# A spectral mixer with a gated token MLP on one core: the order and width of the channel transforms that interrupt the second matrix product

## The chip, the cores and the metric

The kernel runs on one core of one Trainium2 chip. The metric is the device time of one execution in microseconds, as the median of several. The profile is of one execution, taken by the hardware profiler; its times count from the first instruction. TensorE (PE, with its weight loads as PEld), VectorE (DVE), ScalarE (ACT) and GpSimd (POOL) are the engines that compute; SyncE (SP) and POOL issue most of the DMAs.

## What is computed

The input x has 2048 tokens of 512 channels, all in fp32. It is normalized per token, and two branches start from the result.

```python
xn = _layernorm(x, axis=-1)
# branch A: a filter in the 2D spectrum
X = jnp.fft.rfft2(xn, axes=(-2, -1)) * (w_r + 1j * w_i)
s = jnp.fft.irfft2(X, s=(S, D), axes=(-2, -1))
# branch B: an MLP over the tokens
h = _layernorm(xn, axis=-1)
u = gelu(jnp.einsum("bsd,sf->bdf", h, w1) + b1)          # F = 1792
y = jnp.einsum("bdf,fs->bds", u, w2) + b2
g = silu(y.transpose(0, 2, 1))
return x + s * g
```

Here `S` is 2048, `D` is 512, and the two weights of the MLP are 2048x1792 and 1792x2048.

## The kernel before

The Fourier transforms are matrix products with small constant matrices. The kernel has three stages on TensorE, which follow each other without a pause:

- up to about 84 us the first part of the first MLP product, with the forward token transform between its matmuls;
- up to about 204 us the rest of that product, with the channel transform, the filter and the first step of the way back, eight steps of `filter_pair`; what is left of the spectral branch then stands in the tile `ey`;
- from 204.47 us the second MLP product, with the last two transforms of the spectral branch.

The change is in the third stage. Tokens are worked off in eight pairs p of 128-token blocks, `j0 = p` and `j1 = p + 8` (loop `for p in range(NP)` near the end). Each pair is computed with Strassen's scheme in seven products, in the order `ORDER = (1, 2, 5, 6, 3, 7, 4)` (line 802). `products(p, n)` (line 906) issues 21 matmuls of 128x128 weights and 256 columns: three for each of seven slices of the hidden dimension, because each fp32 operand is split into a high and a low part. The weights are the tiles `w2f`, which ACT (high part) and DVE (low part) make in `w2_forms`, two or so products ahead; the moving tiles `fa`, `fb`, `fc`, `fd` are combinations of the hidden layer, made earlier. Three PSUM banks take the results (`banks`, line 903): `bx` for products 1, 6, 7 and 4, which accumulate there one after the other, `by` and `bz` for the rest. Between them the bank is read: `c22`, for instance, is the sum of `bx` after product 7 and of an earlier copy `p5`; product 4 then goes on accumulating in `bx`. DVE makes such sums (`summed`, tile `c`), and ACT makes the gates from them (`gate`, tile `g`).

Behind one product of each pair (`k == slot`; k = 5, that is product 7, in pairs 0 to 6, and k = 3, product 6, in the last) the products are interrupted by transforms of the spectral branch. A string of letters in `PARTS` says which, and in what order:

- `E`, `even_channels` (line 966): the even channel frequencies as 32 matmuls of 64x64 (weights `yt`, moving `ci`, which the profile calls `cd`);
- `O`, `odd_channels` (line 977): the odd ones as 8 matmuls of 128x128;
- `F`, `channels` (line 984): even and odd ones as 16 matmuls of 128x128, even ones then at full width also;
- `S`, `spectral` (line 1019): the last token transform, of the pair before, as 8 matmuls of 64x512 (weights `y`, moving `cft`).

`E`, `O` and `F` write banks 6 and 7, `S` writes banks 0 and 1. Their weights `yt` are gathered from `ey` by ACT and DVE (`gathered`) in steps named "g" in the plan `SLOTS`. After the interruption `unfolded(p)` (line 991) makes `y` from banks 6 and 7 in three steps: the first right behind it, the others at the places marked "s" in the plan. If the letters of the pair hold an "E", its first step is one copy of 257 columns on ACT, three short DVE operations and two long ones; otherwise it is one copy of 512 columns on ACT and two long DVE operations. From the second pair on, `finish` (line 1035) multiplies the result of `S` with the gates on DVE, and POOL adds the rows to `out` with accumulating DMAs; `sums_of_blocks` then forms the next weight blocks on DVE.

Nearly all instructions stand in program order on each engine, which the class `Kept` sees to (line 140 in the profile is its helper, so most rows of this stage carry L140). The letters are read here:

```python
                if k == slot:
                    for part in PARTS[p]:
                        {"S": spectral, "E": even_channels, "O": odd_channels, "F": channels}[part](p - (part == "S"))
                    yts.pop(p)
                    pieces = unfolded(p)
                    if p:
                        for g, j in zip(gates.pop(p - 1), (j0 - 1, j1 - 1)):
                            finish(g, j, whole)
```

Of the kernel before, what the change touches and what calls it, by code (L numbers as in the profile page):

```python
# [17 lines left out]
S, D, F = 2048, 512, 1792  # L18
# [22 lines left out]

PARTS = ("EO", "OES", *["ESO"] * 5, "SF")

KD = np.concatenate([np.arange(0, 256, 4), np.arange(2, 256, 4), np.arange(1, 256, 2)])

# [95 lines left out]
def spectral_mixer_kernel(tc, x, w1, b1, w2, b2, wk, we, wx, c_f, c_ft, c_d, c_i, c_g, c_h, c_t, out):  # L143
# [19 lines left out]
    with tc.tile_pool(name="ps", bufs=1, space=PSUM) as psp, ExitStack() as left, ExitStack() as right:  # L163
# [827 lines left out]
        def unfolded(p):  # L991

            es, y = new_sums(p) if p else first_sums
            e0, e1 = (es[:, :, k].rearrange("p i b c -> p i (b c)") for k in range(2))
            if "E" in PARTS[p]:
                first, odd = ps[:, 6, :256].rearrange("p (i s c) -> p i s c", s=2, c=64), ps[:, 6:8, 256:]
# [53 lines left out]
        for p in range(NP):  # L1050
# [8 lines left out]
            for k, n in enumerate(ORDER):  # L1059
# [23 lines left out]
# [3 lines that stand above are left out]
# [57 lines left out]
```

## Time and profile before

| | |
|---|---|
| median of 3 runs | 366.80 us (366.69 to 366.90) |
| the profiled execution's own time | 367.48 us |
| its span, first to last instruction | 365.70 us |
| granted TensorE clock | 1.00 |
| TensorE busy | 359.3 us, 98% of the span |
| VectorE busy | 304.8 us, 83% |
| ScalarE busy | 210.1 us, 57% |
| first product of the third stage | starts at 204.47 us |
| interruption of the first pair | starts at 219.40 us |
| interruption of the second pair | starts at 238.51 us |

A row of the order of time reads: start, length, engine, line, operation, output tile <- input tiles, shape, count. A row merges neighbours of one group, so its length runs from the start of the first to the modelled end of the last; matmuls are pipelined, and a matmul's own duration is longer than the distance to the next one. That is why the text works with differences of starts. Where a row merges two shapes, it shows the first.

### The profile page before, as it was taken

Reading aid. Unit: us, or ns where it says so; the run is one execution under the profiler, and the core shown is the slowest. Engines: PE = TensorE matmul, PEld = TensorE weight load, DVE = VectorE, ACT = ScalarE, POOL = GpSimd, SP = SyncE. Lnnn points to the kernel's source line nnn. Section 1 sums busy time; section 2 is a strip of 40 time slices with the busy share of each in tenths; the row PEclk is TensorE's granted clock in tenths of the full one; section 3 lists DMA queues with packets and bytes.
Section 4 is the critical chain, followed back from the end, with each engine's and each line's share of the span. In section 5 each row is a group of like instructions: output and inputs, shape, how many; then the busy total and the mean of one; then the engine's idle time right before and its main releaser. Section 6 shows DMA issues by size and latency. Waiting matters only on the chain.

```text
span 365.7 us, 8778 instructions
## 1 busy us (share of the span) xinstructions
PE 359.3 (98%) x3442; PEld 309.5 (85%) x3442; DVE 304.8 (83%) x586; ACT 210.1 (57%) x383; POOL 87.1 (24%) x134
## 2 busy tenths in 40 slices
PE   8999999999999999999999999999999999999994
PEld 5788888888777787777888999989898989898983
DVE  5899999947689997999995978787787969696983
ACT  4877677768634425765426875646464545565541
POOL 4233333323221022220111001050403122140330
PEclk9999999999999999999999999999999999999999
DMA  6988899305694676986568278698898989898623
GB/s 203 243 199 203 206 266 343 140 2 135 148 293 183 208 217 181 266 240 208 169 210 194 100 196 204 163 190 207 187 186 215 177 222 159 233 159 232 106 33 83
DMA packets 33449, 68.66 MB, mean 188 GB/s; under 512 B 4768, under 2 KB 19536, under 8 KB 33280
## 3 DMA queue, kind: packets, MB, share of 16 engines
q1 hardware_dynamic: 24432, 42.44, 41.3%
q0 software_dynamic: 8496, 25.01, 31.9%
q10 hardware_dynamic: 480, 0.66, 0.6%
q8 instruction: 27, 0.44, 0.5%
q14 instruction: 14, 0.11, 0.1%
HBM read 59.70 MB, written 8.13 MB: 185 GB/s over the span
## 4 chain that ended last, share of the span: by engine, by line
PE 97%; DVE 1%; DMA 1%; ACT 0%; issue 0%
PE ps L140 97%; DMA x<-in_x_dram 1%; DVE rows L140 0%; DVE stm L245 0%; ACT g L140 0%; DVE h L273 0%; DVE tm L230 0%; ACT sdm L224 0%; DVE mvm L221 0%; DVE nbm L238 0%; DVE rsm L231 0%; DVE r0m L229 0%; DVE v2m L222 0%; DVE v2m L223 0%
## 5 line engine op out<-in xcount | busy, mean ns | idle before, releaser
L140 PE MATMUL ps<-h,w1h 128*128 128x512 f32 x400 | 117.5, 401 | 0.3 <-DVE nbm L238 0.3
L140 PEld LDWEIGHTS ps<-h,w1h 128*128 128x128 f32 x400 | 73.7, 190 | 20.1 <-issue 4.9
L140 PE MATMUL ps<-h,w1l 128*128 128x512 f32 x200 | 68.0, 392 | 0.0
L140 DVE TENSOR_TENSOR w2f<-a,w2f 128x896 fp32r<-128x896 f32 x36 | 39.2, 1089 | 22.0 <-ACT w2f L140 22.0
L140 PEld LDWEIGHTS ps<-h,w1l 128*128 128x128 f32 x200 | 38.0, 190 | 8.3
L140 ACT ACTIVATE w2f<-a 128x896 fp32r<-128x896 f32 x36 | 36.8, 1022 | 12.5 <-PE ps L140 7.9
L140 PE MATMUL ps<-fb,w2f 128*128 128x256 f32 x336 | 41.7, 279 | 0.0
L140 POOL DMA_DIRECT2D s<-in_w_dram x14 | 18.3, 1310 | 96.9 <-DMA s<-in_w_dram 49.0
L140 PE MATMUL ps<-fa,w2f 128*128 128x256 f32 x336 | 41.1, 277 | 0.0
L140 PEld LDWEIGHTS ps<-fb,w2f 128*128 128x128 f32 x336 | 39.6, 188 | 1.7 <-ACT g L140 0.8
L140 PE MATMUL ps<-fc,w2f 128*128 128x256 f32 x336 | 39.8, 277 | 0.0
L140 PEld LDWEIGHTS ps<-fa,w2f 128*128 128x128 f32 x336 | 39.6, 188 | 0.0
L140 PEld LDWEIGHTS ps<-fc,w2f 128*128 128x128 f32 x336 | 39.0, 188 | 0.0
L140 POOL DMA_DIRECT2D out_dram<-r x28 | 23.6, 1278 | 27.6 <-DVE r L140 27.6
L156 ACT ACTIVATE w1h<-w1s 128x512 fp32r<-128x512 f32 x26 | 16.1, 631 | 23.6 <-PE ps L140 10.0
L309 POOL TENSOR_TENSOR ey<-t 128x256 f32<-128x256 f32 x16 | 15.7, 980 | 45.4 <-DVE t L307 45.4
L669 POOL DMA_DIRECT2D xc<-xc x16 | 9.8, 619 | 68.5 <-ACT xc L667 44.8
L140 ACT ACTIVATE w2f<-s 128x896 fp32r<-128x896 f32 x15 | 15.3, 1022 | 13.5 <-PE ps L140 12.5
L471 DVE TENSOR_TENSOR w1l<-w1r,w1h 128x384 fp32r<-128x384 f32 x32 | 20.7, 652 | 0.8 <-ACT w1h L468 0.8
L140 PE MATMUL ps<-fd,w2f 128*128 128x256 f32 x168 | 20.5, 277 | 0.0
L140 ACT ACTIVATE g<-c,b2t 128x256 f32<-128x256 f32 x24 | 12.1, 504 | 14.6 <-DVE c L140 14.6
L269 ACT ACTIVATE h<-x,nbm,rsm 128x256 f32<-128x256 f32 (+1 forms) x34 | 18.3, 591 | 3.5 <-DVE nbm L264 2.5
(132 smaller groups left out, 603.0 us busy)
## 6 DMA issues: line engine op xcount, KB each, us to landing
a<-in_w_dram SPq DMA_DIRECT2D x22, 448.0 KB, 4.1
wt<-in_wk_dram POOLq DMA_DIRECT2D x16, 512.0 KB, 5.6
s<-in_w_dram SPq DMA_DIRECT2D x16, 448.0 KB, 4.3
s<-in_w_dram POOLq DMA_DIRECT2D x16, 448.0 KB, 6.3
w1s<-in_w_dram SPq DMA_DIRECT2D x52, 128.0 KB, 4.1
w1r<-in_w_dram SPq DMA_DIRECT2D x28, 192.0 KB, 5.3
xc<-xc POOLq DMA_DIRECT2D x16, 256.0 KB, 3.0
out_dram<-in_x_dram SPq DMA_DIRECT2D x4, 960.0 KB, 6.9
```

Source lines behind the costliest of these rows:

```text
L140: return lambda *args, **kw: self.keep(operation(*args, **kw))
L156: return A.activation(hi, src, AF.Copy), V.tensor_sub(lo, src, hi.bitcast(F32))
L269: keep(A.activation(to, v, AF.Identity, bias=m["nb"][:, i], scale=m["rs"][:, i, 1:2]))
L309: G.tensor_add(ey[:, 0::3, :, j], a, b)
L471: keep(V.tensor_sub(dst, src, hi.bitcast(F32)))
L669: keep(G.dma_start(*(v.rearrange("p s t c -> p s (t c)") for v in (there[c::2], here[1 - c::2, ::-1]))))
```

## The change

One line. The first pair gets full-width channel transforms (`F`) in place of even, then odd ones (`EO`); the second pair gets even, spectral, odd (`ESO`), as the third to seventh pairs have, in place of odd, even, spectral (`OES`).

```diff
-PARTS = ("EO", "OES", *["ESO"] * 5, "SF")
+PARTS = ("F", *["ESO"] * 6, "SF")
```

With "F" the first pair has no "E" among its letters, so its `unfolded` takes the other branch:

```python
            if "E" in PARTS[p]:
                ...
            else:
                pe = ps[:, 6:8].rearrange("p i (h k) -> p i h k", h=2)
                A.activation(e1, pe[:, :, 1], AF.Copy)
                V.tensor_add(e0, pe[:, :, 0], e1)
                V.tensor_sub(e1, pe[:, :, 0], e1)
```

The last pair's letters stay as they are.

## The prediction

> **What bounds the kernel now.** I read the first part of the page, then the chain that ended last, then TensorE's instructions in order of time around the two interruptions that change.
>
> ```profile
> span 365.7 us, 8778 instructions
> PE 359.3 (98%) x3442; PEld 309.5 (85%) x3442; DVE 304.8 (83%) x586; ACT 210.1 (57%) x383; POOL 87.1 (24%) x134
> 6.99 353.74 PE ps L140 x3424
> ```
>
> The last row is from the chain in order of time: from 6.99 us to the tail one unbroken run of matmuls sets the end. So whatever DVE, ACT, POOL or a queue gains or loses counts only if a matmul then waits longer or less. The question is how long TensorE takes, from the start of a product before the interruption to the start of one after it.
>
> ```profile
> 216.84 2.63 PE L140 MATMUL ps<-fb,w2f 128*128 128x256 f32 x21
> 219.40 1.78 PE L140 MATMUL ps<-cd,yt 64*64 64x64 f32 x40
> 221.09 2.74 PE L140 MATMUL ps<-fb,w2f 128*128 128x256 f32 x21
> 223.67 2.64 PE L140 MATMUL ps<-fd,w2f 128*128 128x256 f32 x21
> ...
> 236.03 2.63 PE L140 MATMUL ps<-fb,w2f 128*128 128x256 f32 x21
> 238.51 1.68 PE L140 MATMUL ps<-cd,yt 128*128 128x128 f32 x40
> 240.00 1.04 PE L140 MATMUL ps<-y,cft 64*64 64x512 f32 x8
> 240.97 2.65 PE L140 MATMUL ps<-fb,w2f 128*128 128x256 f32 x21
> 243.46 0.73 PE L140 MATMUL ps<-fd,w2f 128*128 128x256 f32 x5
> ```
>
> These are the first pair's interruption (even then odd: 32 small and 8 full-width matmuls under one row, x40) and the second pair's (odd, even, then spectral x8). A later pair has the order that the second is to get:
>
> ```profile
> 255.36 2.54 PE L140 MATMUL ps<-fb,w2f 128*128 128x256 f32 x21
> 257.83 0.69 PE L140 MATMUL ps<-cd,yt 64*64 64x64 f32 x32
> 258.35 1.04 PE L140 MATMUL ps<-y,cft 64*64 64x512 f32 x8
> 259.32 1.16 PE L140 MATMUL ps<-cd,yt 128*128 128x128 f32 x8
> 260.24 2.63 PE L140 MATMUL ps<-fb,w2f 128*128 128x256 f32 x21
> 262.70 2.54 PE L140 MATMUL ps<-fd,w2f 128*128 128x256 f32 x21
> ```
>
> The second thing to see is that the same matmuls are not equally fast in the two stretches. Six products (126 matmuls of 256 columns) lie between two interruptions:
>
> ```profile
> 223.67:238.39 14.72, 14.72 (x127) 14.72 (x126) 12.05 (x18) 8.41 (x13) 0.88 (x1) 1.00 0.72 165
> 262.70:276.87 14.17, 14.17 (x128) 14.17 (x126) 11.64 (x16) 8.44 (x13) 3.23 (x4) 1.00 0.86 174
> ```
>
> Columns: stretch, its length, then busy time (count) of PE, PEld, DVE, ACT, POOL, and the granted clock, 1.00 in both. Each stretch runs from the first start to the last of its 126 (the counts hold one or two more, in flight at its start), so the spacing is 14.72/125 = 117.8 ns in the second pair and 14.17/125 = 113.4 ns in the fourth, 4.4 ns apart, with no wait shown in either. The wide spacing holds before and after the first interruption (219.40 - 216.84 = 2.56 with the change of shape; 226.14 - 223.67 = 2.47 a product, the 226.14 in the row below); it ends at the second one, where 243.46 - 240.97 = 2.49 still holds a long first matmul, and the fourth pair then has 2.38 a product.
>
> ```profile
> 226.14 2.64 PE L140 MATMUL ps<-fa,w2f 128*128 128x256 f32 x21
> ```
>
> I call these the wide and the narrow spacing. What switches it the trace does not say, and the change touches exactly the two interruptions near the switch.
>
> **The change, part by part.**
>
> *First pair.* Out go 32 small and 8 full-width matmuls, in come 16 full-width ones: 24 matmuls and 24 weight loads fewer.
>
> ```profile
> 238.51 1.05 PE L140 MATMUL ps<-cd,yt 128*128 128x128 f32 x8
> 350.29 2.05 PE L140 MATMUL ps<-cd,yt 128*128 128x128 f32 x16
> 352.10 1.16 PE L140 MATMUL ps<-fa,w2f 128*128 128x256 f32 x8
> ...
> L140 PE MATMUL ps<-cd,ey x128: 270/275/275, 87.3 to 168.9; 128*128 128x128 f32 x128
> ```
>
> Eight of the full-width ones last 1.05 us, of which the last one's own duration is 0.275 (median of the last row's form); the 7 spacings are 0.775/7 = 111 ns. The last pair's sixteen run 352.10 - 350.29 = 1.81 us, entered from small matmuls. Entry: from a product into small matmuls took 2.56 us from the product's start, into full-width ones 238.51 - 236.03 = 2.48, at the same spacing; so the first of the sixteen starts at 216.84 + 2.48 = 219.32, the sixteenth at 219.32 + 15 x 0.111 = 220.99. The product behind an odd block followed its last matmul by 0.03 us (259.32 + 1.16 - 0.275 = 260.21, then 260.24). TensorE could go on at 221.02 instead of 221.09: 0.07 us sooner. But the product behind the interruption accumulates into the bank that the sum c22 reads:
>
> ```profile
> 220.62 0.41 DVE L140 TENSOR_TENSOR c<-ps,p 128x256 f32<-128x256 f32 x1
> ```
>
> c22 ends at 221.03, and the product starts 0.06 later, at 221.09. What stands ahead of c22 on DVE (a weight split from 219.28 that waited 1.55 us for ACT, and c12) is not touched. So the wait takes the gain: **0.00**. Bounds: at best -0.10 (0.07, and 0.03 since a product that follows without a pause has a shorter first step: 262.70 - 260.24 = 2.46 there against 2.49 at 240.97), at worst +0.12 (if the last pair's 1.81 us counted from 219.40: 221.21). I take 0.00, nearest to the c22 row.
>
> The Trainium skill (TensorEngine Tiling, "Available Configurations" and "Theoretical Speedup") speaks against this edit: products of 64 by 64 run as four independent tiles, and giving that up costs time. By the rows it does, 32 small ones in 258.35 - 257.83 = 0.52 us against 8 x 0.111 = 0.89; the two changes of shape that fall away and c22's wait are why the sum above still comes out at nothing, and by the rule alone it would be +0.37.
>
> The unfolding that follows takes the path of the last pair. ACT copies 128x512 in place of 128x257, DVE loses three short operations and keeps two long ones:
>
> ```profile
> L140 ACT ACTIVATE es<-ps x1: 598/598/598, 352.4 to 352.4; 128x512 f32<-128x512 f32 x1
> L140 ACT ACTIVATE y<-ps 128x257 f32<-128x257 f32 x7 | 2.7, 385 | 3.4 <-PE ps L140 3.4
> L140 DVE TENSOR_TENSOR es<-ps,y x14: 277/344/415, 223.2 to 339.2; 128x256 f32<-128x256 f32 x7, 128x128 f32<-128x128 f32 x7
> L140 DVE TENSOR_TENSOR es<-y,ps x7: 273/274/275, 223.7 to 339.4; 128x128 f32<-128x128 f32 x7
> 223.92 1.02 ACT L140 ACTIVATE w2f<-s 128x896 fp32r<-128x896 f32 x1 [1.08 <-issue]
> ```
>
> ACT: +0.598 - 0.385 = +0.21 us, which fits into the 1.08 us it stood idle before the next weight split. DVE: -(2 x 0.344 + 0.274) = -0.96 us. The sums of weight blocks behind it move up by most of that, so later splits and loads start no later. TensorE waited for none of them in this stretch (14.72 of 14.72 busy), so **0.00**. Without that cover the ACT copy would cost its 0.21.
>
> *Second pair.* The same 48 matmuls in another order.
>
> ```profile
> 230.17 0.68 DVE L140 TENSOR_TENSOR y<-es 128x512 f32<-128x512 f32 x1
> 241.11 0.39 ACT L140 ACTIVATE y<-ps 128x257 f32<-128x257 f32 x1 [0.50 <-PE ps L140]
> ...
> 260.52 0.39 ACT L140 ACTIVATE y<-ps 128x257 f32<-128x257 f32 x1 [0.57 <-PE ps L140]
> ```
>
> Before: 243.46 - 236.03 = 7.43 us from the product ahead to the second product behind. A later pair with the new order: 262.70 - 255.36 = 7.34. Between the two lie 20 + 20 spacings; the product ahead is wide here and narrow there, 20 x 4.4 ns = 0.09. So the order itself costs the same: **0.00**, bounds +/-0.02 from the rounding. The moved spectral part issues no DMA; it stands in front of the odd part rather than last, and its y has been written by 230.85. Behind the interruption the copy of the even part comes later: from the start of the product ahead 260.52 - 255.36 = 5.16 us in place of 241.11 - 236.03 = 5.08, of which 0.09 was the wide spacing, so 0.17 later. The products with the gates, the POOL queue's accumulating stores and the next block's load issued there stand behind it on their engines and move by no more; in the later pairs all of them stand so, and TensorE waits for none (14.17 of 14.17 busy).
>
> *Spacing.* I assume that it switches where it does now, behind the second interruption: **0.00**. The new order contains all that the old one did there, and in the later pairs that order is followed by narrow spacing each time. Both other outcomes are rivals. [...]
>
> **Sum**: 0.00 on the profiled execution's 367.48 us (span 365.70 and 1.78 around it); that execution lies 0.68 above the median of the runs, 366.80, so the forecast is **366.8 us**.
>
> **Rivals.**
> (1) *The narrow spacing starts one pair early.* In the later pairs a product that follows full-width channel matmuls at once is narrow; sixteen of them, without small ones between, may set that state already in the first pair. Gain: 20 + 126 = 146 matmuls x 4.4 ns = 0.64 us, 0.74 with the 0.10 above: 366.1 to 366.2. For: the 260.24 row. Against: odd channels preceded the 221.09 product also, it had to wait for c22 as it will now, and it stayed wide (2.47 a product from 223.67).
> (2) *The wide spacing is not ended* (the slower side). If the state is ended by the small matmuls running straight into a product, as the spectral part does at 240.00 to 240.97, the new order has none of that until the last pair: there a spectral part stands directly ahead of the last product. In every later pair odd channels stand between. Price: 20 matmuls of the second pair, 5 x 147, and 126 of the last: 881 x 4.4 ns = 3.9 us: 370.7. It decides as soon as the first product behind the second interruption stays wide. For: the switch is seen once, with the old order. Against: the new order still goes from full width to small and back, at 257.83 and 259.32 in the row's pair, and if that empties TensorE of what went before, the second pair goes on as the later ones do.
> (3) *The first part does nothing at all* is my forecast for it; that it gains its 0.10 because c22 no longer holds gives 366.7 and stays inside the same range.
>
> **How the numbers follow.** Forecast 0.61; rival 1 0.25; rival 2 0.13; 0.01 for a loss that I don't see. A measurement of this kernel can tell about 0.2% (0.73 us) from no change: 366.07 to 367.53. Rival 1 straddles the lower bound, 0.10 of its 0.25 below it. So faster 0.10, same 0.76, slower 0.14. The range takes the forecast with its bounds (366.7 to 366.92, and 0.3 for the runs' own spread and the rounding of the spacings) and rival 1: 365.9 to 367.2; rival 2 stays out.
>
> **What would show it.** First step right: full-width channel matmuls x16 near 219.3, the product behind them still near 221.09, directly after c22. Second: from the product ahead to the second product behind 7.43 us, or 7.34 if the product ahead is narrow. Spacing: the six products behind the first interruption 14.7 us (forecast) or 14.2 (rival 1); those behind the second 14.2 (forecast) or 14.7 in every pair (rival 2). The forecast is wrong if a row of weight loads shows a new wait of TensorE for ACT or DVE there, or if the spacing switches elsewhere.

## The result, and the profile after

| | before | after |
|---|---|---|
| median | 366.84 us (21 runs, 366.12 to 367.60) | 370.17 us (21 runs, 366.13 to 372.13) |
| ratio | | 1.0053 (95%: 1.0034 to 1.0071) |
| profiled execution, own time | 367.48 us | 366.37 us |
| its span | 365.70 us | 364.60 us |

The times after fall into two groups: eight from 366.13 to 367.35 us, one at 368.04, and twelve from 370.08 to 372.13. Those of before lie in one. The ratio leaves out the two longest runs as disturbed; it lies between the groups and describes neither. The profiled execution of the changed kernel belongs to the lower group. Its first part of the page, and the run of matmuls from the chain:

```profile
span 364.6 us, 8727 instructions
PE 358.0 (98%) x3418; PEld 308.4 (85%) x3418; DVE 304.8 (84%) x583; ACT 211.4 (58%) x383; POOL 87.1 (24%) x134
9.55 350.05 PE ps L140 x3391
```

TensorE still sets the end, with 24 matmuls fewer. The two interruptions, from TensorE's order of time:

```profile
203.35 2.64 PE L140 MATMUL ps<-fd,w2f 128*128 128x256 f32 x21
...
215.72 2.63 PE L140 MATMUL ps<-fb,w2f 128*128 128x256 f32 x21
218.19 1.95 PE L140 MATMUL ps<-cd,yt 128*128 128x128 f32 x16
219.97 2.74 PE L140 MATMUL ps<-fb,w2f 128*128 128x256 f32 x21
222.55 2.63 PE L140 MATMUL ps<-fd,w2f 128*128 128x256 f32 x21
...
234.91 2.63 PE L140 MATMUL ps<-fb,w2f 128*128 128x256 f32 x21
237.48 0.69 PE L140 MATMUL ps<-cd,yt 64*64 64x64 f32 x32
237.99 1.04 PE L140 MATMUL ps<-y,cft 64*64 64x512 f32 x8
238.96 1.16 PE L140 MATMUL ps<-cd,yt 128*128 128x128 f32 x8
239.88 2.63 PE L140 MATMUL ps<-fb,w2f 128*128 128x256 f32 x21
242.34 0.84 PE L140 MATMUL ps<-fd,w2f 128*128 128x256 f32 x6
```

The sum c22 of the first pair, from DVE's order of time, and the next weight split on ACT:

```profile
219.50 0.41 DVE L140 TENSOR_TENSOR c<-ps,p 128x256 f32<-128x256 f32 x1
222.79 1.04 ACT L140 ACTIVATE w2f<-s 128x896 fp32r<-128x896 f32 x1 [0.87 <-ACT es L140]
```

And the stretches of six products behind the first, the second and the sixth interruption (length first, then busy time of each engine, with TensorE's first):

```profile
222.55:237.27 14.72, 14.72 (x128) 14.72 (x126) 11.32 (x16) 8.42 (x13) 1.17 (x2) 1.00 0.72 167
242.35:256.51 14.16, 14.16 (x127) 14.16 (x126) 11.62 (x15) 8.41 (x13) 3.17 (x4) 1.00 0.87 176
319.31:333.47 14.16, 14.16 (x127) 14.16 (x126) 11.63 (x16) 8.39 (x13) 3.23 (x4) 1.00 0.88 184
```

This execution went as forecast. From the product ahead of the first interruption to the second one behind it: 222.55 - 215.72 = 6.83 us, before 223.67 - 216.84 = 6.83; c22 ends at 219.91, and the product follows 0.06 us later, as before. At the second: 242.34 - 234.91 = 7.43, before 7.43. The spacing is wide up to the second interruption (14.72) and narrow behind it (14.16). What makes the upper group is not in this profile, so the first experiment runs the changed kernel again, to profile an execution of that group.

### The profile page after: what moved, and what is told of

Same layout as the page of the kernel before. It is cut to its first block, busy times and chain, and to the rows that moved or that the text cites. A ratio compares the mean times of both kernels' runs of the same rounds, so it can differ in the third digit from the quotient of the medians.

```text
span 364.6 us, 8727 instructions
## 1 busy us (share of the span) xinstructions
PE 358.0 (98%) x3418; PEld 308.4 (85%) x3418; DVE 304.8 (84%) x583; ACT 211.4 (58%) x383; POOL 87.1 (24%) x134
## 4 chain that ended last, share of the span: by engine, by line
PE 96%; DVE 1%; DMA 1%; ACT 0%; issue 0%
PE ps L140 96%; DMA x<-in_x_dram 1%; DVE stm L245 0%; ACT h L269 0%; DVE rows L140 0%; DVE h L471 0%; ACT g L140 0%; DVE h L273 0%; DVE tm L230 0%; ACT sdm L224 0%; DVE mvm L221 0%; DVE r0m L229 0%; DVE rsm L231 0%; DVE nbm L238 0%; DVE v2m L222 0%
## 5 line engine op out<-in xcount | busy, mean ns | idle before, releaser
L140 PEld LDWEIGHTS ps<-h,w1h 128*128 128x128 f32 x400 | 72.8, 188 | 20.5 <-issue 4.9
```

The lines of the kernel that those rows point to most:

```text
L140: return lambda *args, **kw: self.keep(operation(*args, **kw))
```

## The experiments

All were timed beside runs of the kernel before on the same chip, whose medians lay between 366.84 and 367.00 us.

**The changed kernel again, and its parts alone.** Kernels: the change once more; its second part alone; its first part alone; the change with the first pair's interruption as odd, even.

```diff
-PARTS = ("F", *["ESO"] * 6, "SF")                # the change again
+PARTS = ("EO", *["ESO"] * 6, "SF")               # order alone
+PARTS = ("F", "OES", *["ESO"] * 5, "SF")         # width alone
+PARTS = ("OE", *["ESO"] * 6, "SF")               # small ones last
```

> The changed kernel once more. Its times fell into two groups, 366.1 to 368.0 and 370.1 to 372.1 us. Theory W (my rival 2, but by chance of the execution): in the upper group the interruption in the order even, spectral, odd does not end the wide spacing, so all pairs up to the last spectral part run at 117.8 ns; a run of the upper group has 14.7 us in each stretch of six products, and 881 x 4.4 ns = 3.9 us more than the lower group. Theory C (clock or start): the upper group loses its 3.9 us before 204 us or shows a granted clock below 1 in the third stage; the stretches stay 14.2 us from the second pair on. Both expect times in both groups.

> Only the second part of the change: the first pair even, odd as before; the second even, spectral, odd. Theory W: two groups as with the whole change, about 366.8 and 370.5. Rival F (the sixteen full-width matmuls of the first pair bring the wide spacing to stay): one group at 366.8.

> Only the first part: full-width channel matmuls in the first pair, the second pair odd, even, spectral as before. Theory W: one group at 366.8, narrow from the product behind the second interruption. Rival F: two groups.

> The first pair's interruption as odd, even: the small matmuls run straight into the product, without a spectral part; the others as in the changed kernel. Theory W1 (the change of shape straight into a product ends the wide spacing): narrow from 221 us on, 146 x 4.4 ns = 0.64 us less than before, 366.2, one group. Theory W2 (the spectral part itself ends it, if it stands last): nothing ends it in the first pair, two groups at 366.8 and 370.5.

| kernel | up to 367.7 us | between | from 369.9 us | median |
|---|---|---|---|---|
| the change again | 6 | 2 | 4 | 367.88 |
| order alone | 7 | 1 | 4 | 367.22 |
| width alone | 7 | 5 (368.26 to 369.85) | 0 | 367.08 |
| small ones last | 8 | 1 | 3 | 367.09 |

The profile of the change again was of the upper group (370.06 us). Its stretches behind the first, the second and the sixth interruption, and its second interruption in order of time:

```profile
222.27:236.99 14.72, 14.72 (x127) 14.72 (x126) 11.32 (x16) 8.40 (x13) 1.13 (x2) 1.00 0.72 168
242.16:256.88 14.72, 14.72 (x127) 14.72 (x126) 11.66 (x16) 8.42 (x13) 3.09 (x4) 1.00 0.85 176
321.71:336.43 14.72, 14.72 (x128) 14.72 (x126) 11.65 (x16) 8.40 (x13) 3.06 (x4) 1.00 0.85 177
```

```profile
203.08 2.16 PE L140 MATMUL ps<-fd,w2f 128*128 128x256 f32 x17
...
234.64 2.63 PE L140 MATMUL ps<-fb,w2f 128*128 128x256 f32 x21
237.20 0.69 PE L140 MATMUL ps<-cd,yt 64*64 64x64 f32 x32
237.72 1.04 PE L140 MATMUL ps<-y,cft 64*64 64x512 f32 x8
238.69 1.16 PE L140 MATMUL ps<-cd,yt 128*128 128x128 f32 x8
239.60 2.72 PE L140 MATMUL ps<-fb,w2f 128*128 128x256 f32 x21
```

The wide spacing never ends, at a granted clock of 1.00 and with the same work on the other engines. The span is 368.3 us. From the first product of the third stage to the end this is 368.3 - 203.08 = 165.2 us, in the lower group's profile 364.6 - 203.35 = 161.2: 4.0 us, against 881 x 4.4 ns = 3.9. So the upper group is the wide spacing, kept to the end, and theory C falls. Even the last product stays wide, though a spectral part runs straight into it; its 21 matmuls, and below them the same ones of the kernel before:

```profile
359.52 1.09 PE L140 MATMUL ps<-y,cft 64*64 64x512 f32 x8
360.54 2.74 PE L140 MATMUL ps<-fb,w2f 128*128 128x256 f32 x21
...
358.06 2.65 PE L140 MATMUL ps<-fb,w2f 128*128 128x256 f32 x21
```

The difference is 20 spacings of 4.4 ns.

It hangs on the second part of the change: the new order alone has the upper group, the width alone has none. Yet the width alone is not quite as the kernel before either: in its profile the old order did not end the wide spacing, and the third pair's interruption did.

```profile
223.85:238.57 14.72, 14.72 (x127) 14.72 (x126) 11.33 (x16) 8.41 (x13) 1.45 (x2) 1.00 0.71 170
243.74:258.46 14.72, 14.72 (x127) 14.72 (x126) 11.60 (x16) 8.39 (x13) 3.10 (x4) 1.00 0.86 177
263.54:277.70 14.16, 14.16 (x127) 14.16 (x126) 11.61 (x15) 8.42 (x13) 3.15 (x4) 1.00 0.85 180
```

Small matmuls straight ahead of the product, without a spectral part, end nothing in the first pair (W1 falls): behind the odd, even of "small ones last" the six products take 14.72 us.

```profile
223.66:238.38 14.72, 14.72 (x127) 14.72 (x126) 12.05 (x18) 8.42 (x13) 0.84 (x1) 1.00 0.69 161
```

But in the width alone small matmuls with a spectral part last did not end it either, nor did the spectral part ahead of the upper group's last product (W2 as it stood falls).

**A rhythm.** The views round to 10 ns; the trace keeps starts to 1 ns. Take the 147 matmuls of 256 columns between two interruptions, count their spacings from the end, and sort them by place modulo three (some 48 of each place). The wide ones of the upper group's profile are then 118.33, 117.33 and 117.66 ns on average. So every third spacing is a long one, and in this profile it is the last one, the fourth last and so on at each interruption up to the last product's. As a pair has 147 = 3 x 49 matmuls, the rhythm comes to each interruption at the same beat; beat here means whether the last, the second last or the third last spacing ahead of the interruption is the long one. The first four experiments and the two kernels sort themselves by the beat at which the interruption is met:

```
long spacing at the end of the run   order                 spacing behind
last          (kernel before)        odd, even, spectral   narrow
second last   (width alone)          odd, even, spectral   wide
third last    (4 profiles)           even, spectral, odd   narrow
last          (upper group, 6 times) even, spectral, odd   wide, long spacing last again
```

In all six profiles the first interruption was met with the long spacing last; the beat behind it differed. What could differ from execution to execution there is the wait for c22. This became theory R, and the next runs move the beat by adding matmuls, or take the wait away.

**Two or three further matmuls in the third pair.** They go to the bank that the even channels overwrite.

```diff
                     T.matmul(o, wf[:, wi, i], form_parts(n, i)[ui], ...
+            if n == 7 and p in (2,):
+                for i in FORMS[:2]:          # FORMS[:3] in the other kernel
+                    T.matmul(ps[:, 6, :HD], wf[:, 1, i], form_parts(n, i)[0], start=True, stop=True)
```

> The changed kernel with two further 256-column matmuls at the end of product 7 of the third pair, into the bank that the even channels overwrite. Theory R (rhythm): wide spacings come in a rhythm of three (118.33, 117.33, 117.66 ns means in the profile of the upper group), a pair's 147 matmuls are a multiple of three, so an execution that meets the interruption at the wrong beat meets every later one at the same beat and stays wide to the end; in the four profiles that left the wide spacing at even, spectral, odd the long spacing stood third from the end, in the one that stayed it was the last. Two further matmuls move it from last to third from the end: such executions leave at the third pair. No time near 370; at most 0.65 + 0.23 us above the lower group, so 366.3 to 368.2. Rival I (each execution or each program has a fixed property, no rhythm): a group at 370.3.

> As before, with three further matmuls in the same place: a whole turn of the rhythm. Theory R: the beat is unchanged, two groups, 366.5 and 370.5 (0.34 us for the three). Rival S (any further matmuls, or their store to another bank, break the state): one group near 366.5 to 368.

With two, none of twelve reached 369.2 us (366.26 to 369.12, median 367.82). With three, one of twelve lay in the upper group (370.52), eight up to 367.14 and three from 368.04 to 368.32. That agrees with R, but one is few. The profiles added a third beat that I had not met: with the long spacing second last, even, spectral, odd stays wide, but the next pair is met with it third last and lets go. In the profile of the kernel with two, they moved such an execution back from third to second last, so it was let go one pair later still; it took 368.00 us, with a span of 366.0. The three times above the 368.2 expected (368.85 to 369.12) are not explained by that alone: their mean granted clock was 0.993 to 0.994, that of the other nine 0.996 or more (where such runs lose time stands at the end of the next section).

**No wait for c22.** One weight split of the first pair is taken behind c22 on ACT and DVE; first with sixteen full-width matmuls, then with even, odd.

```diff
-                if not started:
+                if not started and (p or n != 3):
+                    if not p and n == 7:
+                        ready.append(next(wforms))
                     ready.extend(w for w in [next(wforms, None)] if w is not None)
```

> The changed kernel with one weight split of the first pair moved behind c22 on ACT and DVE, so that product 4 need not wait for c22. Theory R with the wait as the source of chance: the six products ahead of the first interruption had the same beat in all six profiles, and the wait for c22 on another engine is what makes the beat behind it differ; without it all executions behave alike: one group, either 366.1 (narrow from the first pair on), 366.8, or 370.3. Rival I: two groups as before.

> The same move of the split with the first pair as even, odd and the second as even, spectral, odd. Theory R: one group (366.1, 366.8 or 370.3). Rival I: two groups.

Measured: 366.64 to 368.31 us (median 367.01) and 366.51 to 367.66 (median 366.69), no upper group in twelve each. The first kernel's order of time, c22 from DVE's and the rest from TensorE's:

```profile
215.60 2.63 PE L140 MATMUL ps<-fb,w2f 128*128 128x256 f32 x21
218.07 1.95 PE L140 MATMUL ps<-cd,yt 128*128 128x128 f32 x16
219.77 2.72 PE L140 MATMUL ps<-fb,w2f 128*128 128x256 f32 x21
222.33 0.87 PE L140 MATMUL ps<-fd,w2f 128*128 128x256 f32 x6
```

```profile
218.34 0.43 DVE L140 TENSOR_TENSOR c<-ps,p 128x256 f32<-128x256 f32 x1 [1.53 <-PE ps L140]
```

c22 is done at 218.77, a full microsecond ahead of the product; 222.33 - 215.60 = 6.73 us in place of 6.83. Both profiles met the second interruption with the long spacing second last, stayed wide for that pair, and let go at the third interruption.

**The beat set by hand.** With the wait gone (even, odd in the first pair), further matmuls at the end of product 7: two in the first pair, or one or two in the second.

```diff
+            if n == 7 and p == 0:            # p == 1 in the two others
+                for i in FORMS[:2]:          # FORMS[:1] in one of them
+                    T.matmul(ps[:, 6, :HD], wf[:, 1, i], form_parts(n, i)[0], start=True, stop=True)
```

> The kernel of the last run (c22 ahead of the split; even, odd; then even, spectral, odd), with two further matmuls at the end of product 7 of the first pair. The first interruption is met with the long spacing last in every profile; two more put it third from the end, where four interruptions were left narrow. Theory R: narrow from the first pair on, one group; against the last run 147 + 147 + 20 matmuls x 4.4 ns = 1.4 us less and 0.23 us more, 365.5. If even, odd alone does not let go at that beat: one group, wide for one or two pairs, 366.0 to 367.6.

> The same kernel with one further matmul at the end of product 7 of the second pair, none in the first. There the long spacing stood second from the end; one more puts it third. Theory R: narrow from the second interruption on in place of the third, 0.65 us less and 0.12 more than without it: one group at 366.15. Rival (the execution decides, not the count): as without it, 366.8.

> The same with two further matmuls there instead of one. Theory R: the long spacing then is the last one at the second interruption and at every later one: wide to the end in all executions, 734 matmuls x 4.4 ns = 3.2 us and 0.23 more than without them, one group at 370.2. Rival: 366.9 (only the two matmuls' time) or two groups.

One further matmul in the second pair gives 366.24 us (12 runs: nine from 366.05 to 366.55, three from 367.47 to 367.64), two give 370.37 (370.24 to 371.70, all 4 runs): 4.1 us for one matmul of 0.12. The stretches around the second interruption of the kernel with one, then of the kernel with two (the first stretch of each holds the further matmuls), and the sixth of the latter:

```profile
223.43:238.36 14.93, 14.93 (x129) 14.93 (x128) 11.36 (x16) 8.40 (x13) 1.27 (x2) 1.00 0.70 170
243.44:257.60 14.16, 14.16 (x127) 14.16 (x126) 11.54 (x15) 8.42 (x13) 3.07 (x4) 1.00 0.85 180
```

```profile
222.32:237.38 15.06, 15.06 (x131) 15.06 (x129) 11.48 (x16) 8.44 (x13) 1.74 (x2) 1.00 0.73 174
242.54:257.26 14.72, 14.72 (x127) 14.72 (x126) 11.44 (x16) 8.41 (x13) 2.87 (x4) 1.00 0.83 178
322.09:336.81 14.72, 14.72 (x127) 14.72 (x126) 11.65 (x16) 8.41 (x13) 3.05 (x4) 1.00 0.87 175
```

The medians met both forecasts of R, to 0.2 us. The profile with one is of its three longest runs (367.47 us); it is narrow from the second interruption on all the same, and its third stage starts over 1.1 us later than the changed kernel's, at 204.50. The kernel with two also removes rival S: further matmuls with their store to the other bank do not by themselves end the wide spacing. None, one and two further matmuls have thus met the second interruption at the three beats and had three outcomes; three, which should do as none, were not run without c22's wait. Two further matmuls in the first pair (366.91 us, 366.76 to 368.32, 11 runs) did not make it narrow there, so R's 365.5 was missed and the other forecast, 366.0 to 367.6, met by all but one run: even, odd does not let go at the third beat; it passes the run on with the long spacing second last, and the third interruption of that execution let go.

**The old order at the third beat.**

```diff
-PARTS = ("EO", *["ESO"] * 6, "SF")
+PARTS = ("EO", "OES", *["ESO"] * 5, "SF")        # with one further matmul in the second pair
```

> The kernel with one further matmul in the second pair, but with the second interruption in the old order odd, even, spectral. The long spacing stands third from the end there. The question is why the kernel before has no upper group although it waits for c22 too: its order let go in its profile with the long spacing last, and did not with it second from the end (the run with the first part alone). If it also lets go at the third beat, one group at 366.2, and the old order never meets a beat at which it is caught for good. If it does not: one group wide for a pair more, 366.8, or to the end, 370.

One group, 366.61 to 366.99 us (median 366.80). The old order stays wide at this beat, and the pair behind it lets go:

```profile
242.11:256.84 14.73, 14.73 (x127) 14.73 (x126) 11.49 (x16) 8.41 (x13) 3.10 (x5) 1.00 0.84 177
261.92:276.08 14.16, 14.16 (x127) 14.16 (x126) 11.62 (x15) 8.43 (x13) 3.13 (x4) 1.00 0.84 177
```

Over all fourteen profiles, the interruptions met at the wide spacing from the second pair on:

```
long spacing   even, spectral, odd                      odd, even, spectral
last           12 times wide, next time last again      once narrow
second last     6 times wide, next time third last      once wide, next time third last
third last     11 times narrow                          once wide, next time third last
```

(Next time: without further matmuls between. The 12 times come from two profiles, the 11 from eleven; each entry of the right column is one interruption of one profile.) By this table the kernel before can have no upper group. It waits for c22 too, but its old order lets go at the one beat at which the new order holds for good, and hands the others on to a later pair at the beat at which the new order lets go: at most one pair's 0.65 us is lost. With the new order in the second pair nothing catches the first case. The runs of the kernel before agree, as far as times can: none on record lies above 368.44 us, and of the 35 beside the first four experiments eight have spans of 364.2 to 364.7 us, 21 of 364.9 to 365.4, one pair's 0.65 apart. By that most executions of before let go a pair later than the profiled one did; one profile alone does not show it.

That the wait for c22 deals the beats shows behind the first interruption. In the eight profiles with the wait the products up to the second interruption end with the long spacing last twice, second last three times and third last three times; in the six without it, further matmuls of the second pair taken off, it is second last each time.

## Why the prediction was wrong

*The first pair, 0.00 for sixteen full-width matmuls behind c22's wait.* Right: 6.83 us both times, with the product 0.06 us behind c22, and without the wait 6.73, the lower bound of -0.10.

*The unfolding, 0.00.* Right: no matmul waited for it (14.72 of 14.72 us busy behind it), and the next weight split started 0.24 us after the second product behind (222.79 - 222.55), before 0.25 (223.92 - 223.67).

*The new order itself, 0.00.* Right: 7.43 us in the profile before and in the one after.

*"Spacing. I assume that it switches where it does now".* This step failed. I read one execution of before, in which all later pairs are narrow behind the new order, as evidence that this order makes the spacing narrow. Those pairs were narrow already when they came to it; it only kept them so. Coming from the wide spacing, it lets go at one beat of three, at another it stays wide for good, and the wait for c22 sets the beat anew in each execution. What came in place of the assumed switch is 14.72 us instead of 14.2 in every pair, some 900 matmuls x 4.4 ns = 4.0 us, in about half of the executions. So the kernel has no single time: in 33 runs, 16 lay from 369.9 us up. That the median fell into the upper group is chance: 12 of 21 runs lay there, and in the second batch, 4 of 12, the median was 367.88. The profiled execution agrees with the forecast row by row and would have hidden the wrong step.

*Rival 2* had the price right (3.9 us, measured 4.0) and its place (the first product behind the second interruption), but the cause wrong: not whether small matmuls run straight into a product, which at the second and third beat ended nothing in the old order, and at the last beat nothing ahead of the upper group's last product. And it is not one outcome of the program but of the execution; I gave it 0.13. *Rival 1* did not come about: behind sixteen full-width matmuls the spacing was wide in the profiles, with the wait and without it.

Left open: what in TensorE makes the two spacings and the rhythm of three; and why c22's wait gave the last beat in about half of the runs of the change but once in twelve with three further matmuls (on another chip than the repeat of the change). Very little may decide. In the seven profiles with the wait and with even, odd or sixteen full-width matmuls in the first pair, the step from the last product matmul ahead of the interruption to the first one behind is 1894 to 1896 ns; the two with 1894 came out at the last beat, the five with 1895 or 1896 at another. With a resolution of 1 ns that shows no cause.

The longer times inside the groups are older than the third stage. In four of the fourteen profiles (the kernel before, the width alone, small ones last, one further matmul in the second pair) the first six matmuls of the first MLP product take 2.6 to 2.9 us, in the other ten 1.6 to 1.7, and the third stage starts at 204.4 to 204.7 us instead of 203.0 to 203.4. The row of the width alone, its granted clock a little later (third number from the end), and the row of the changed kernel:

```profile
7.25 2.63 PE L140 MATMUL ps<-h,w1h 128*128 128x512 f32 x6 [1.67 <-DVE nbm L238]
9.00:11.00 2.00, 2.00 (x7) 1.54 (x6) 1.90 (x7) 1.08 (x3) 1.20 (x4) 0.51 1.08 245
...
7.16 1.66 PE L140 MATMUL ps<-h,w1h 128*128 128x512 f32 x6 [0.45 <-DVE nbm L238]
```

Between 7 and 11 us the granted clock reads 0.51 to 0.64 in three of the four, but 1.00 in that of before. With this the span of the width alone is accounted for: 364.6 us of the lower group's profile, 1.3 for the late start of the stage (204.66 against 203.35) and 0.65 for one pair more of wide spacing make 366.6. Its two longest runs (369.31 and 369.85 us) have spans of only 366.7 and 366.9; the rest of their time lies outside the span.

The kernel with one further matmul in the second pair and without c22's wait is the best of these: 366.24 against 366.84 us of before beside it; the ratio's interval, 0.9989 (0.9975 to 1.0004), just reaches 1.

## What to carry to other kernels

Where TensorE is busy all the time, compare the spacing of equal matmuls between stretches before counting what else an edit moves: here 4.4 ns of 118 decided 4 us. A state that a profile shows behind an interruption may have been there ahead of it; look for an interruption that was entered in the other state before taking it as a cause. And profile the same program more than once where its times fall into groups: the median of two groups is no time of either.

## What the runs showed that was not expected

The same 128x128 weights and 256 columns have two stable spacings, 117.8 and 113.3 ns, at a granted clock of 1.00. The wide one is there from the first 256-column product behind the 512-column stage in all fourteen profiles. Either can outlast interruptions of 8 to 48 other matmuls with two or more changes of shape: the narrow one did so every time, the wide one at two beats of three in the new order. The number of matmuls modulo three set the outcome (none more: 366.69 us, one more: 366.24, two more: 370.37).
